# A delta-rule attention with its triangular inverse rearranged: transposes in place of paired products, and a new order of steps

## The chip, the core and the metric

The kernel runs on one core of a Trainium2 chip. A core has a matrix engine (TensorE, in the trace PE for its matmuls and PEld for its weight loads), VectorE (DVE), ScalarE (ACT), GpSimd (POOL) and SyncE (SP), which mostly issues DMAs. Each engine runs its own list of instructions in order and waits for the others by semaphores. Matmuls write to PSUM, eight banks of 128 partitions by 512 fp32 numbers, and DVE or ACT must copy a result from there to SBUF before the matrix engine can use it again. The metric is the device time of one execution in microseconds.

## What is computed

```python
k_n = k / (np.linalg.norm(k, axis=-1, keepdims=True) + 1e-06)
for t in range(S):
    kt, vt, bt = (k_n[:, :, t], v[:, :, t], beta[:, :, t, None])
    y[:, :, t] = np.einsum('bhd,bhde->bhe', q[:, :, t], state)
    v_old = np.einsum('bhde,bhd->bhe', state, kt)
    state = state + bt[:, :, :, None] * np.einsum('bhd,bhe->bhde', kt, vt - v_old)
...
logits = xn @ en.T / tau                      # 8 experts, the best one is taken
h = np.maximum(x[mask] @ w1[e], 0.0)
out[mask] = gate_w[mask, None] * (h @ w2[e])
```

The attention has 4 batches, 8 heads, 768 tokens and head size 48. Its output, 3072 rows of 384, is routed row by row to one of eight experts with 1024 hidden units.

## The kernel before

The recurrence is cut into chunks of 64 tokens. Within a chunk the updates of the state form a triangular system of 64 by 64 for each head, and the kernel inverts its matrix with products. A **unit** is one chunk of two batches: the one batch lies on partitions 0 to 63, the other on 64 to 127, and the 8 heads lie side by side, so that a matrix of a unit is a tile of 128 by 512. There are 24 units (12 chunks, 2 pairs of batches).

A unit passes these steps. `prep` normalises K on POOL and DVE (the roots are `pow` on POOL, L269 and L275). `transposes` makes K and Q transposed. `gram` makes the products K·K and Q·K. The inverse starts with blocks of 8 (`square_t`, `square`, `fourth`, `first_w`) and doubles the block size three times: `level` (L389 copies the lower part out of PSUM under a mask) and `grow`, which makes both W and its transpose T by two products, and at the end `last`. `k_state` and `q_state` read the running state, `solve` applies W, `state` adds to the running state, `outputs` makes the rows of the result, `x_transposes` and `logits` prepare the routing. After every fourth unit `route` sorts the rows to experts.

Every matmul of these steps is 64 by 64 (or 48) by 64 and uses one quarter of the array: rows 0 to 63 or 64 to 127, columns 0 to 63 or 64 to 127. `product` issues two matmuls for each head, one for each batch, on two quarters that lie diagonally (`from_other` and `to_other` choose which diagonal).

What sets the order on the matrix engine is the table `PLAN` with `PERIOD = 8`: each step of unit n has the due time 8·n plus its number, all are sorted, and steps with the same due time are interleaved matmul by matmul (the loop at L578 to L589). So in the running stage two products on different diagonals go side by side. The other engines' lists are left to the scheduler. PSUM has one pool `bank` of six buffers and one `yb` of two.

After the attention, the expert stage (from L595) takes the rows expert by expert in 31 tiles of 128 rows: a gather, 24 matmuls with `w1`, ReLU, 8 with `w2`, and an indirect store. Its weights come by DMA from SP.

Of the kernel before, what the change touches and what calls it, by code (L numbers as in the profile page):

```python
# [8 lines left out]
F32 = mybir.dt.float32  # L9
# [8 lines left out]
LEVELS = (8, 16, 32)  # L18
BLOCK = 8
# [3 lines left out]
def kernel(  # L23
# [33 lines left out]

    nc = tc.nc
# [9 lines left out]
    ps = ctx.enter_context(tc.tile_pool(name="ps", bufs=1, space=bass.MemoryType.PSUM))  # L68
# [3 lines left out]
    def bank(shape):  # L72
        return ps.tile(shape, F32, name="bank", tag="bank", bufs=6)

    def yb():
        t = ps.tile([128, 512], F32, name="yb", tag="yb", bufs=2)
        return t[:, 0:NP * D].rearrange("p (j d) -> p j d", j=NP)
# [32 lines left out]
    att = ExitStack()  # L110
# [35 lines left out]
    id2 = ac.tile([128, 1, C], F32, name="id2")  # L146
    nc.vector.tensor_scalar_mul(id2, id64, 2.0)
    nupper = ac.tile([128, 1, C], F32, name="nupper")
    nc.vector.tensor_tensor(nupper[:, 0, :], col_f, trow_f, op=ALU.is_gt)
    lower = ac.tile([128, C], F32, name="lower")  # L150
    nc.vector.tensor_tensor(lower, col_f, trow_f, op=ALU.is_lt)

    def mask(name, tri, lo, hi):
        m = ac.tile([128, 1, C], F32, name=name)
        nc.vector.scalar_tensor_tensor(out=m[:, 0, :], in0=xor_f, scalar=float(lo), in1=tri,
                                       op0=ALU.is_ge, op1=ALU.mult)
        nc.vector.scalar_tensor_tensor(out=m[:, 0, :], in0=xor_f, scalar=float(hi), in1=m[:, 0, :],
                                       op0=ALU.is_lt, op1=ALU.mult)
        return m.bitcast(I32)

    up8 = mask("up8", nupper[:, 0, :], 0, BLOCK)
    lo8 = mask("lo8", lower, 0, BLOCK)
    below = {s: mask(f"below{s}", lower, s, 2 * s) for s in LEVELS}
    nc.vector.tensor_scalar_mul(nupper, nupper, -1.0)
    hc = [128, H, C]


    def filled(name, bufs, value):

        ts = []  # L170
        for i in range(bufs):
            t = ac.tile(hc, F32, name=f"{name}{i}")
            if value is None:
                nc.gpsimd.memset(t, 0.0)
            elif value == 1.0:
                nc.vector.tensor_copy(t, id64.broadcast_to(hc))
            else:
                nc.vector.tensor_scalar_mul(t, id64.broadcast_to(hc), value)
            ts.append(t)
        return ts  # L180

    KK = filled("KK", 8, None)
    Qp = [filled(f"Qp{i}_", NU, None) for i in range(2)]
    YT = filled("YT", 3, -1.0)
    YI = filled("YI", 2, 1.0)
# [7 lines left out]
    def load_kq(c):  # L193
        K4 = io.tile([128, NU, H, D], F32, name="K4", tag="K4")
        for b in range(B):
            p, u = slice(b % 2 * C, b % 2 * C + C), b // 2
            for dst, src in ((K4[p, u], k), (Qp[c % 2][u][p, :, 0:D], q)):
                nc.sync.dma_start(out=dst, in_=src[b, :, c * C:(c + 1) * C, :].rearrange("h p d -> p h d"))
        return K4

    def load_v(c):
        V4 = io.tile([128, NU, H, D], F32, name="V4", tag="V4", bufs=4)
        for b in range(B):
            p, u = slice(b % 2 * C, b % 2 * C + C), b // 2
            nc.sync.dma_start(out=V4[p, u], in_=v[b, :, c * C:(c + 1) * C, :].rearrange("h p d -> p h d"))
        return V4

    bt = ac.tile([B * H, S], F32, name="bt")
# [5 lines left out]
    K4s, V4s = {0: load_kq(0)}, {}  # L214
# [35 lines left out]

    HALF = (slice(0, C), slice(C, 2 * C))
    UNITS = [dict(n=n, c=n // NU, u=n % NU) for n in range(NC * NU)]
    sqb = {}
    outs = {}

    def hs():
        return range(H)

    def work(name, bufs=2, cols=C):
        return wk.tile([128, H, cols], F32, name=name, tag=name, bufs=bufs)

    def prep(U):
# [5 lines left out]
        K = K4s[c][:, u]  # L270
# [8 lines left out]
        U["K"] = KK[U["n"] % len(KK)]  # L279
        nc.gpsimd.tensor_tensor(U["K"][:, :, 0:D], K, rn.unsqueeze(2).broadcast_to([128, H, D]), op=ALU.mult)  # L280

    def scale_v(U):
        V = V4s[U["c"]][:, U["u"]]
        nc.gpsimd.tensor_tensor(V, V, sqb[U["c"]][:, U["u"]].unsqueeze(2).broadcast_to([128, H, D]), op=ALU.mult)
        U["R"] = V

    def transposes(U):
        U["KT"] = wk.tile([128, NP, 2, 128], F32, name="KT", tag="KT", bufs=6)
        for i, src in enumerate((U["K"], Qp[U["c"] % 2][U["u"]])):
            psT = bank([128, NP, 128])  # L290
            for j in range(NP):
                nc.tensor.transpose(psT[:, j, :], src[:, 2 * j:2 * j + 2, :].rearrange("p h d -> p (h d)"), ident)
            nc.scalar.activation(U["KT"][:, :, i, :], psT, ACT.Copy)

    def gram(U):

        KT, ps = U["KT"], [bank([128, 2, NP, C]) for _ in range(2)]
        groups = []
        for j in range(NP):
            for a in range(2):  # L300
                g = []
                for jj in range(2):
                    pr = slice(jj * C, jj * C + D)
                    for i in range(2):
                        g.append((ps[jj][HALF[i if a else 1 - i], a, j], KT[pr, j, 0, HALF[i]],
                                  KT[pr, j, a, HALF[i]], True))
                groups.append(g)

        def after():
            n = U["n"]  # L310
            U["G"] = wk.tile([128, 2, 2, NP, C], F32, name="G", tag="G", bufs=6)
            U["YT"], U["YI"] = YT[n % len(YT)], YI[n % len(YI)]
            for jj in range(2):
                js = slice(jj * NP, jj * NP + NP)
                nc.scalar.activation(U["G"][:, :, jj], ps[jj], ACT.Copy, scale=-1.0)  # L315
                for t, m in ((U["YT"], up8), (U["YI"], lo8)):
                    nc.vector.copy_predicated(t[:, js], m.broadcast_to([128, NP, C]), ps[jj][:, 0])  # L317
            U["A"] = U["G"][:, 0].rearrange("p jj j t -> p (jj j) t")
            U["M"] = U["G"][:, 1].rearrange("p jj j t -> p (jj j) t")
            nc.gpsimd.tensor_tensor(U["M"], U["M"], nupper.broadcast_to(hc), op=ALU.mult)  # L320
        return groups, after

    def product(p, lhsT, rhs, from_other, to_other):

        groups = []
        for h in hs():
            g = []
            for i in range(2):
                f, o = HALF[1 - i if from_other else i], HALF[1 - i if to_other else i]
                g.append((p[o, h], lhsT[f, h], rhs[f, h], True))  # L330
            groups.append(g)
        return groups

    def evac(eng, out, p):
        if eng == "act":
            nc.scalar.activation(out, p, ACT.Copy)  # L336
        else:
            nc.vector.tensor_copy(out, p)

    def square(U):  # L340
        p = bank(hc)

        def after():
            U["Y2"] = work("Y2")
            nc.vector.tensor_tensor(U["Y2"], p, id2.broadcast_to(hc), op=ALU.add)
        return product(p, U["YT"], U["YI"], True, True), after

    def square_t(U):
        p = bank(hc)

        def after():
            U["Y2T"] = work("Y2T")
            evac("act", U["Y2T"], p)
        return product(p, U["YI"], U["YT"], True, True), after

    def fourth(U):
        p = bank(hc)

        def after():
            U["P"] = work("Y4")  # L360
            nc.vector.tensor_tensor(U["P"], p, id2.broadcast_to(hc), op=ALU.add)
        return product(p, U["Y2T"], U["Y2"], True, False), after

    def first_w(U):
        p = bank(hc)

        def after():
            U["W"] = work("W", 5)
            nc.scalar.activation(U["W"], p, ACT.Copy, scale=-1.0)
        return product(p, U["Y2"], U["YT"], True, False), after  # L370

    def grow(U, eng_w="act"):
        pt, pw = bank(hc), bank(hc)
        P, W = U["P"], U["W"]
        gt, gw = product(pt, W, P, False, True), product(pw, P, W, False, False)

        def after():
            U["T"] = work("T", 3)
            evac("act", U["T"], pt)
            U["W"] = work("W", 5)  # L380
            evac(eng_w, U["W"], pw)
        return [g for gs in zip(gt, gw) for g in gs], after

    def level(U, s):
        p = bank(hc)

# [324 lines left out]
```

## Time and profile before

| | |
|---|---|
| time before, median of 3 runs | 971.53 us (964.52 to 976.65) |
| the profiled execution's own time | 977.07 us |
| its span, first to last instruction | 975.3 us |
| PE matmul busy | 736.1 us, 75%, 18598 instructions |
| PE weight loads | 18598 instructions |
| DVE, ACT, POOL busy | 270.4, 246.2, 262.8 us |
| mean granted TensorE clock | 0.912 of 2.4 GHz |

The profile is of one execution. A wait that is put down to "issue" is one for which the trace shows no semaphore and no other engine's work. A row of a timeline merges neighbouring instructions of one kind; the number behind x counts them. In the trace an fp32 matmul of the source is two MATMUL rows, each with a weight load (LDWEIGHTS) of its own; a transpose is one of each. The trace can miss a few matmul records.

### The profile page before, as it was taken

To read this page: it belongs to the slowest core of one execution; us is meant where nothing else is said; L and a number is where in the kernel's file an instruction comes from. 1 tells how busy PE (TensorE), PEld (TensorE's weight loads), DVE (VectorE), ACT (ScalarE), POOL (GpSimd) and SP (SyncE) were. 2 spreads that over 40 slices of the span, in tenths; PEclk is the share of its full clock that TensorE was granted. 3 is DMA by queue.
4 is the path that set the end of the run, shared out by engine and by line. 5 is a ranking of instruction groups with operands and counts; after the bars stand their busy time and mean duration, and the time that the engine had idled before them with its cause. 6 is when DMAs were issued, how large, how long until landed. Compare 5 with 4: busy or idle time off the path is not lost. (4 is left out here: it accounts for less than half of the span.)

```text
span 975.3 us, 40125 instructions
## 1 busy us (share of the span) xinstructions
PE 736.1 (75%) x18598; PEld 633.3 (65%) x18598; DVE 270.4 (28%) x742; ACT 246.2 (25%) x503; POOL 262.8 (27%) x252
## 2 busy tenths in 40 slices
PE   0476767667667667776876770399999999999995
PEld 0366766667666666665765660377887788877884
DVE  7234434424343435324433322000100010001000
ACT  0233433333432434344333330010011001100110
POOL 6977144252423223211200101111121121111110
PEclk9987999878997999799889895599999999999998
DMA  5232121211222122110100101999999999999960
GB/s 92 48 61 52 27 38 29 60 27 29 45 46 34 29 45 49 24 20 4 37 4 5 36 3 33 372 326 324 322 322 333 325 321 323 327 315 328 318 201 1
DMA packets 135449, 130.13 MB, mean 133 GB/s; under 512 B 85738, under 2 KB 120721, under 8 KB 135282
## 3 DMA queue, kind: packets, MB, share of 16 engines
q1 hardware_dynamic: 128738, 116.55, 39.7%
q0 software_dynamic: 4736, 10.85, 3.3%
q8 instruction: 146, 2.39, 1.1%
q10 hardware_dynamic: 1808, 0.16, 0.1%
q14 instruction: 21, 0.17, 0.1%
HBM read 117.91 MB, written 10.95 MB: 132 GB/s over the span
## 5 line engine op out<-in xcount | busy, mean ns | idle before, releaser
L660 PE MATMUL bank<-xTm,w 128*128 128x128 f32 x1488 | 173.8, 277 | 0.0
L660 PEld LDWEIGHTS bank<-xTm,w 128*128 128x128 f32 x1488 | 171.3, 194 | 0.3
L665 PE MATMUL bank<-w,hT 128*128 128x384 f32 x496 | 165.1, 486 | 0.0
L665 PEld LDWEIGHTS bank<-w,hT 128*128 128x128 f32 x496 | 91.9, 190 | 57.5
L662 ACT ACTIVATE hT<-bank 128x512 f32<-128x512 f32 x62 | 37.0, 597 | 338.5 <-PE bank L660 283.7
L588 PE MATMUL bank<-T,G 64*64 64x64 f32 x2304 | 103.3, 240 | 18.8 <-issue 17.7
L588 PE MATMUL bank<-W,P 64*64 64x64 f32 x2304 | 98.0, 231 | 23.2 <-issue 22.6
L588 PEld LDWEIGHTS bank<-T,G 64*64 64x64 f32 x2304 | 89.8, 152 | 22.8 <-issue 21.0
L667 DVE TENSOR_SCALAR y<-bank,xg 128x384 f32<-128x384 f32 x31 | 19.1, 617 | 305.6 <-PE bank L665 305.6
L588 PEld LDWEIGHTS bank<-W,P 64*64 64x64 f32 x2304 | 84.9, 144 | 28.8 <-issue 27.0
L336 ACT ACTIVATE T<-bank 128x512 f32<-128x512 f32 x72 | 43.1, 598 | 167.6 <-PE bank L588 162.7
L588 PE MATMUL bank<-P,W 64*64 64x64 f32 x1536 | 67.0, 234 | 17.0 <-issue 15.8
L668 POOL DMA_INDIRECT out_dram<-y,ids x31 | 31.3, 1011 | 164.3 <-DVE y L667 161.5
L389 DVE COPY_PREDICATED P<-below,bank 128x512 f32<-128x512 int32 x72 | 53.0, 736 | 71.3 <-PE bank L588 62.3
L588 PEld LDWEIGHTS bank<-P,W 64*64 64x64 f32 x1536 | 58.6, 147 | 20.1 <-issue 18.8
L641 POOL DMA_INDIRECT xg<-x_dram,ids x31 | 30.1, 971 | 136.9 <-DMA ids<-idmap 92.6
L320 POOL TENSOR_TENSOR G<-G,nupper 128x512 f32<-128x512 f32 x24 | 30.5, 1271 | 133.0 <-ACT G L315 122.8
L549 POOL DMA_INDIRECT idmap<-tokid,slot_i x24 | 24.0, 1000 | 107.5 <-DMA idmap<-tokid,slot_i 57.9
L317 DVE COPY_PREDICATED YT<-up,bank 128x256 f32<-128x256 int32 x48 | 21.2, 442 | 98.8 <-ACT G L315 98.8
L588 PE MATMUL bank<-Y,W 64*64 64x64 f32 x768 | 37.3, 253 | 14.8 <-issue 11.2
L588 PE MATMUL bank<-KT 48*64 48x64 f32 x1536 | 38.2, 243 | 11.3 <-issue 10.9
L275 POOL TENSOR_TENSOR rn<-rn,half 128x8 f32<-128x8 f32 x24 | 39.5, 1646 | 24.8 <-DVE rn L274 24.1
(167 smaller groups left out, 1255.2 us busy)
## 6 DMA issues: line engine op xcount, KB each, us to landing
w<-in_moe_w_dram SPq DMA_DIRECT2D x62, 1536.0 KB
x_dram<-xc SPq DMA_DIRECT2D x24, 192.5 KB
K<-in_k_dram SPq DMA_DIRECT2D x48, 96.0 KB
V<-in_v_dram SPq DMA_DIRECT2D x48, 96.0 KB
Qp<-in_q_dram SPq DMA_DIRECT2D x48, 96.0 KB
ids<-idmap SPq DMA_DIRECT2D x31, 0.5 KB
xg<-x_dram,ids POOLq DMA_INDIRECT x31, 6.7
out_dram<-y,ids POOLq DMA_INDIRECT x31, 6.9
```

The lines of the kernel that those rows point to most:

```text
L275: nc.gpsimd.tensor_tensor(out=rn, in0=rn, in1=half[:, 0], op=ALU.pow)
L317: nc.vector.copy_predicated(t[:, js], m.broadcast_to([128, NP, C]), ps[jj][:, 0])
L320: nc.gpsimd.tensor_tensor(U["M"], U["M"], nupper.broadcast_to(hc), op=ALU.mult)
L336: nc.scalar.activation(out, p, ACT.Copy)
L389: nc.vector.copy_predicated(U["P"], below[s].broadcast_to(hc), p)
L549: nc.gpsimd.indirect_dma_start(out=idmap[:, :], out_offset=bass.IndirectOffsetOnAxis(ap=slot_i[:, g:g + 1], axis=0), in_=tokid[:, c - 1 + ...
L588: nc.tensor.matmul(out_, lhsT=lhsT, rhs=rhs, start=start, stop=True, skip_group_check=True)
L641: nc.gpsimd.indirect_dma_start(out=x, out_offset=None, in_=x_dram[:, :], in_offset=bass.IndirectOffsetOnAxis(ap=ids[:, 0:1], axis=0))
L660: nc.tensor.matmul(psH[:, i, :], lhsT=w1[:, j, (f + i) * 128:(f + i + 1) * 128], rhs=xT[:, j, :], start=(j == 0), stop=(j == KC - 1))
L662: nc.scalar.activation(hT[:, f:f + 4, :], psH, ACT.Relu)
L665: nc.tensor.matmul(psO, lhsT=hT[:, f, :], rhs=w2[:, f, :], start=(f == 0), stop=(f == NF - 1))
L668: nc.gpsimd.indirect_dma_start(out=out[:, :], out_offset=bass.IndirectOffsetOnAxis(ap=ids[:, 0:1], axis=0), in_=y, in_offset=None, bounds_ ...
```

## The change

The inverse now starts at blocks of 2 instead of 8: `square_t`, `square`, `fourth` and `first_w` are gone, and W starts from `gram`'s result under a mask. There are four levels (2, 4, 8, 16) instead of three. `grow` makes W alone; T, its transpose, comes from four transposes of 128 by 128 (`t_flip`), and A is transposed once in the same way (`a_flip`). The last doubling, to 64, is not made; the right-hand side is solved in three steps instead (`solve1`, `solve2`, `solve3`). `gram` makes both of its products in one matmul with 128 columns. `product` now uses all four quarters of the array within one step (two heads, two batches), into two banks. Steps are no longer interleaved; the plan gives each of the 24 slots of a period one step, and steps that write to `pair` (three buffers of two banks) alternate with steps that write to `bank` (two buffers of one bank). K, Q and V are loaded per unit instead of per chunk. The expert stage gets a PSUM pool of its own, `acc`, with eight buffers.

```diff
-LEVELS = (8, 16, 32)
-BLOCK = 8
+LEVELS = (2, 4, 8, 16)
...
-        return ps.tile(shape, F32, name="bank", tag="bank", bufs=6)
+        return ps.tile(shape, F32, name="bank", tag="bank", bufs=2)
+    def pair(shape):
+        t = ps.tile([128, 2, 512], F32, name="pair", tag="pair", bufs=3)
...
+    def load(U, dst, src):
+        t0 = U["c"] * C
+        for i in range(2):
+            nc.sync.dma_start(out=dst[i * C:(i + 1) * C],
+                              in_=src[2 * U["u"] + i, :, t0:t0 + C, :].rearrange("h p d -> p h d"))
...
+        KT, p = U["KT"], pair([NP, 2, C])
         for j in range(NP):
+            for jj in range(2):
+                pr = slice(jj * C, jj * C + D)
+                for i in range(2):
+                    mm(p[HALF[i], jj, j], KT[pr, j, 0, HALF[i]], KT[pr, j, :, HALF[i]])
...
+    def flip(src):
+        p = bank(jc)
+        for j in range(NP):
+            nc.tensor.transpose(p[:, j].rearrange("p r c -> p (r c)"), src[:, j].rearrange("p r c -> p (r c)"), ident)
+        return p
+    def a_flip(U):
+        p = flip(U["A"][0])
+        U["A"][1] = work("AJ", 3)
+        nc.scalar.activation(U["A"][1], p, ACT.Copy)
+        U["T"] = T2[U["n"] % 2]
+        nc.vector.copy_predicated(U["T"], below[1].broadcast_to(jc), p)
+    def t_flip(U, eng):
+        p = flip(U["W"])
+        U["T"] = work("T", 3)
+        eng(U["T"], p)
...
+    def product(lhsT, rhs):
+        p = pair([NP, C])
+        for j in range(NP):
+            for a in range(2):
+                for b in range(2):
+                    mm(p[HALF[b], a, j], lhsT[HALF[a], j, b], rhs[HALF[a], j, b])
...
+    def grow(U):
+        p = product(U["P"], U["W"])
+        U["W"] = work("W", 5)
+        act_copy(U["W"], p)
...
+    def apply(lhsT, rhs):
+        p = bank([128, H, D])
+        for h in range(H):
+            for i in range(2):
+                mm(p[HALF[i], h], lhsT[HALF[i], h // 2, h % 2], rhs[HALF[i], h])
+        return p
+    def solve1(U):
+        p = apply(U["W"], U["R"])
+        U["Z1"] = narrow("Z1")
+        nc.scalar.activation(U["Z1"], p, ACT.Copy, scale=first)
+    def solve2(U):
+        p = apply(U["A"][0], U["Z1"])
+        nc.vector.scalar_tensor_tensor(out=U["R"], in0=p, scalar=second, in1=U["R"], op0=ALU.mult, op1=ALU.add)
+    def solve3(U):
+        p = apply(U["W"], U["R"])
+        U["Z"] = narrow("Z")
+        act_copy(U["Z"], p)
...
-    PERIOD = 8
+    PERIOD = 24
     PLAN = [
-        (-24, prep), (8, scale_v), (-19.5, transposes), (-15.5, gram),
-        (-10, square_t), (-6, square), (-3, fourth), (0, first_w), (3, grow),
-        (6, lambda U: level(U, 8)), (9, grow), (12, lambda U: level(U, 16)), (15, lambda U: grow(U, "dve")),
-        (18, lambda U: level(U, 32)), (21, last), (21.5, k_state), (23.5, q_state), (24, solve),
-        (26.5, state), (28, outputs), (31.5, x_transposes), (33.5, logits),
+        (-72, load_kq), (-42, prep), (-30, load_v), (10, scale_v),
+        (-23, lambda U: transposes(U, 0)), (-19, lambda U: transposes(U, 1)), (-12, gram), (-5, a_flip),
+        (0, lambda U: level(U, 2, 1)), (4, grow), (9, lambda U: t_flip(U, nc.vector.tensor_copy)),
+        (14, lambda U: level(U, 4, 0)), (18, grow), (23, lambda U: t_flip(U, nc.vector.tensor_copy)),
+        (30, lambda U: level(U, 8, 1)), (34, grow), (39, lambda U: t_flip(U, act_copy)),
+        (44, lambda U: level(U, 16, 0)), (50, grow),
+        (32, q_state), (40, k_state), (55, solve1), (59, solve2), (65, solve3), (70, state), (69, outputs),
+        (75, x_transposes), (85, logits), (90, route_after),
     ]
```

First place: the matrix engine's list in the running stage of the attention, a part of a unit's period. Of before (W and P are the inverse and its next factor, YT and Y belong to the start of a later unit, S and KT to `q_state`, R to `solve`; x counts matmuls of the source):

```order
L588 MATMUL bank<-P_1_190,W 64x64 x2
L588 MATMUL bank<-W,P_1_190 64x64 x2
...
L482 MATMUL bank<-ident,xc 128x128 x3
L588 MATMUL yb<-S_196,KT 64x48 x16
L588 MATMUL bank<-R,W 64x48 x2
L588 MATMUL bank<-YT_176,Y_5602 64x64 x2
...
L588 MATMUL bank<-KT 64x64 x32
```

And of the change (a row with `ident` is a block of transposes, `W,P` is `grow`, `T,AJ` or `T,G` is `level`, `R,W` is `solve1` or `solve3`, `Z_1897,G` is `solve2`):

```order
L268 MATMUL pair<-W,P_1_196 64x64 x16
L444 MATMUL bank<-ident,xc 128x128 x3
L268 MATMUL pair<-W_1_176,P_1_184 64x64 x16
L304 MATMUL bank<-ident,QQ_170 128x128 x4
L268 MATMUL pair<-T,AJ 64x64 x16
L268 MATMUL bank<-R,W 64x48 x16
L268 MATMUL pair<-S_198,KT 64x48 x16
L329 MATMUL bank<-ident,W 128x128 x4
L268 MATMUL pair<-W,P_0_190 64x64 x16
L268 MATMUL bank<-Z_1897,G 64x48 x16
L268 MATMUL pair<-KT 64x128 x16
```

The alternation of two products is gone: each step stands alone, the products with R, W and Z among them, and a block of transposes stands between products about every fourth row.

Second place: VectorE's list in the running stage. Of before (P is `level`'s masked copy, Y belongs to the start of a unit, the rn rows are `prep`):

```order
L274 TENSOR_REDUCE rn<-Ksq 128x8
L276 TENSOR_SCALAR rn<-rn 128x8
L277 RECIPROCAL rn<-rn 128x8
L278 TENSOR_TENSOR rn<-rn,sqb 128x8
L389 COPY_PREDICATED P_0_188<-below_143,bank 128x512
L361 TENSOR_TENSOR Y_5309<-bank,id_128 128x512
```

And of the change:

```order
L342 COPY T<-bank 128x512
L286 TENSOR_REDUCE rn<-Ksq 128x8
L359 COPY_PREDICATED P_0_182<-below_138,pair 128x512
L288 TENSOR_SCALAR rn<-rn 128x8
L289 RECIPROCAL rn<-rn 128x8
L290 TENSOR_TENSOR rn<-rn,sqb 128x8
L359 COPY_PREDICATED P_1_192<-below_144,pair 128x512
L342 COPY T<-bank 128x512
L406 SCALAR_TENSOR_TENSOR R<-bank,second,R 128x384
```

In both lists one masked copy stands directly behind the rn rows, of which the second waits for POOL's `pow`. In the change another masked copy stands between the sum of squares and that wait.

## Rows read from the trace of the kernel before

**Rows 1.** Windows: us, PE, PEld, DVE, ACT, POOL busy (x), clock, DMA, GB/s.
```profile
100.00:540.00 440.00, 311.68 (x13818) 284.30 (x13812) 169.46 (x456) 168.47 (x360) 116.84 (x103) 0.90 0.16 30
...
627.00:975.30 348.30, 338.51 (x2073) 271.05 (x2071) 33.16 (x61) 37.04 (x62) 59.51 (x60) 0.99 0.87 294
```

**Rows 2.** Waits of PE in 100:540: us in total, times, longest.
```profile
PE bank L588 <- issue: 95.9, 88, 3.2
PE yb L588 <- issue: 16.2, 16, 2.5
PE bank L535 <- DVE den L524: 9.3, 4, 2.7
PE bank L588 <- DVE P L389: 2.5, 2, 1.3
```

**Rows 3.** DMA queues in 100:540: packets, MB, share of 16 engines.
```profile
q8 instruction: 108, 1.77, 1.8%
```

**Rows 4.** Windows cut where a PE wait for "issue" ends.
```profile
500.70:504.46 3.76, 2.13 (x128) 2.00 (x128) 0.00 (x0) 0.98 (x2) 0.00 (x0) 1.00 0.02 4
504.46:508.03 3.57, 3.34 (x127) 3.06 (x128) 1.49 (x5) 2.06 (x4) 1.28 (x1) 0.74 0.02 5
...
511.88:515.62 3.74, 2.08 (x128) 1.96 (x128) 1.44 (x2) 1.66 (x5) 0.00 (x0) 1.00 0.02 4
...
519.64:523.11 3.47, 2.72 (x128) 2.35 (x128) 0.69 (x1) 1.81 (x4) 0.00 (x0) 1.00 0.02 5
```

**Rows 5.** Costliest groups by line: xcount, then busy us, mean ns, idle before.
```profile
L588 PE MATMUL bank<-T,G 64*64 64x64 f32 x2304 | 103.3, 240 | 18.8 <-issue 17.7 <-DVE W L338 1.0
L389 DVE COPY_PREDICATED P<-below,bank 128x512 f32<-128x512 int32 x72 | 53.0, 736 | 71.3 <-PE bank L588 62.3 <-PE yb L588 8.7
L336 ACT ACTIVATE T<-bank 128x512 f32<-128x512 f32 x72 | 43.1, 598 | 167.6 <-PE bank L588 162.7 <-PE bank L482 4.9
L275 POOL TENSOR_TENSOR rn<-rn,half 128x8 f32<-128x8 f32 x24 | 39.5, 1646 | 24.8 <-DVE rn L274 24.1 <-DVE rn L278 0.8
...
L667 DVE TENSOR_SCALAR y<-bank,xg 128x384 f32<-128x384 f32 x31 | 19.1, 617 | 305.6 <-PE bank L665 305.6
...
L292 PE MATMUL bank<-ident,KK 128*128 128x128 f32 x96 | 17.9, 311 | 17.1 <-POOL KK L280 14.8 <-issue 2.2
...
L338 DVE COPY W<-bank 128x512 f32<-128x512 f32 x24 | 16.6, 692 | 33.8 <-PE bank L588 28.4 <-PE bank L482 5.4
```

**Rows 6.** Timeline of PE where steps stand alone: start, us, what, xcount, idle before.
```profile
576.88 0.64 PE L588 MATMUL bank<-S,KT 48*64 48x48 f32 x30
577.45 0.55 PE L482 MATMUL bank<-ident,xc 128*128 128x128 f32 x3
577.92 0.68 PE L588 MATMUL yb<-S,KT 48*64 48x48 f32 x32
578.42 1.17 PE L588 MATMUL bank<-R,W 64*64 64x48 f32 x32
579.52 0.52 PE L588 MATMUL bank<-enT,xT 128*64 128x8 f32 x12
580.26 1.13 PE L588 MATMUL yb<-Z,G 64*64 64x48 f32 x32 [0.22 <-ACT Z L336]
581.93 0.55 PE L482 MATMUL bank<-ident,xc 128*128 128x128 f32 x3 [0.53 <-ACT xc L336]
583.05 0.52 PE L588 MATMUL bank<-enT,xT 128*64 128x8 f32 x12 [0.58 <-ACT xT L484]
```

**Rows 7.** Timeline of PE at a granted clock of 0.5.
```profile
465.43 1.05 PE L588 MATMUL bank<-Z,KK 64*64 64x48 f32 x32
466.26 0.34 PE L588 MATMUL bank<-Y,W 64*64 64x64 f32 x2
```

**Rows 8.** Windows before and at a fall of the granted clock.
```profile
295.00:299.00 4.00, 1.82 (x92) 1.48 (x92) 0.76 (x1) 0.60 (x1) 0.00 (x0) 1.00 0.39 37
299.00:313.00 14.00, 11.94 (x351) 10.78 (x355) 3.41 (x8) 4.35 (x8) 4.81 (x5) 0.58 0.14 23
```

More of the change, by code (lines that the diff above doesn't have):

```diff
@@ L253, with mm, work, narrow @@
     HALF = (slice(0, C), slice(C, 2 * C))
[L254 to L262, printed above, removed]
+    sqb, outs = {}, {}
+    def mm(out_, lhsT, rhs, start=True):
+        nc.tensor.matmul(out_, lhsT=lhsT, rhs=rhs, start=start, stop=True, skip_group_check=True)
+    def work(name, bufs=2):
+        return wk.tile(jc, F32, name=name, tag=name, bufs=bufs)
+    def narrow(name, bufs=2):
+        return wk.tile([128, H, D], F32, name=name, tag=name, bufs=bufs)
     def prep(U):
@@ L279, in prep, with transposes @@
         U["K"] = KK[U["n"] % len(KK)]
+        U["K"] = U["K"].rearrange("p j r d -> p (j r) d")
         nc.gpsimd.tensor_tensor(U["K"][:, :, 0:D], K, rn.unsqueeze(2).broadcast_to([128, H, D]), op=ALU.mult)
     def scale_v(U):
-        V = V4s[U["c"]][:, U["u"]]
+        V = U["R"]
         nc.gpsimd.tensor_tensor(V, V, sqb[U["c"]][:, U["u"]].unsqueeze(2).broadcast_to([128, H, D]), op=ALU.mult)
[L285 to L293, printed above, removed]
+    def transposes(U, a):
+        if a == 0:
+            U["KT"] = wk.tile([128, NP, 2, 128], F32, name="KT", tag="KT", bufs=4)
+        p, src = bank([128, NP, 128]), U["Q" if a else "K"]
+        for j in range(NP):
+            nc.tensor.transpose(p[:, j], src[:, 2 * j:2 * j + 2, :].rearrange("p h d -> p (h d)"), ident)
+        act_copy(U["KT"][:, :, a], p)
@@ L309, in after @@
[L309 to L382, printed above, removed]
@@ L384, in level @@
-    def level(U, s):
-        p = bank(hc)
-        def after():
-            U["P"] = PP[s][U["n"] % 2]
-            nc.vector.copy_predicated(U["P"], below[s].broadcast_to(hc), p)
-        return product(p, U["A"], U["T"], True, False), after
-    def last(U):
-        p = bank(hc)
-        groups = product(p, U["P"], U["W"], False, False)
-        def after():
-            U["W"] = work("W", 5)
-            evac("act", U["W"], p)
-        return groups, after
-    def of_state(U, a):
-        p = [yb() if a else bank([128, NP, D]) for _ in range(2)]
-        groups = []
-        for j in range(NP):
-            g = []
@@ new lines, in level, with by_head, of_state @@
+    def level(U, s, by):
+        p = product(U["A"][by], U["T"])
+        U["P"] = PP[s][U["n"] % 2]
+        nc.vector.copy_predicated(U["P"], below[s].broadcast_to(jc), p)
+    def grow(U):
+        p = product(U["P"], U["W"])
+        U["W"] = work("W", 5)
+        act_copy(U["W"], p)
+    def by_head(t):
+        return t.rearrange("p (j jj) d -> p j jj d", jj=2)
+    def of_state(U, a):
+        p = pair([NP, D])
+        for j in range(NP):
+            for jj in range(2):
+                pr = slice(jj * C, jj * C + D)
+                for i in range(2):
+                    mm(p[HALF[i], jj, j], U["KT"][pr, j, a, HALF[i]], S_u[U["u"]][pr, j, i])
+        return p.rearrange("p jj j d -> p j jj d")
@@ L415, in k_state @@
     def k_state(U):
+        V = U["R"]
+        U["R"] = narrow("R")
         if U["c"] == 0:
[L417 to L425 removed]
@@ L453, in state @@
         S_ = S_u[U["u"]]
-        def after():
-            for i in range(2):
-                nc.vector.tensor_tensor(S_[:, :, i], p[i], S_[:, :, i], op=ALU.add)
-        return groups, after
+        nc.vector.tensor_tensor(S_, p.rearrange("p i j d -> p j i d"), S_, op=ALU.add)
     def outputs(U):
@@ L575 @@
-    events.sort(key=lambda e: e[:2])
-    with tc.manual_schedule(engines={mybir.EngineType.PE}):
-        while events:
-            now = [events.pop(0)]
-            while events and events[0][0] == now[0][0]:
-                now.append(events.pop(0))
-            done = [r for r in (e[2]() for e in now) if r is not None]
-            groups = [g for g, _ in done]
-            while any(groups):
-                for g in groups:
-                    if g:
-                        for out_, lhsT, rhs, start in g.pop(0):
-                            nc.tensor.matmul(out_, lhsT=lhsT, rhs=rhs, start=start, stop=True,
-                                             skip_group_check=True)
-            for _, after in done:
-                after()
+        (-72, load_kq), (-42, prep), (-30, load_v), (10, scale_v),
```

209 lines of the change are left out of this document (95 added, 114 removed).

## The prediction, made before the changed kernel was run

> **What bounds the kernel now.** I first cut the span into stages. From 100 to 540 us the attention runs full: PE is busy 311.68 of 440 us, DVE 169.46, ACT 168.47 and POOL 116.84, so none of the four fills the stage [rows 1]. The expert stage after 627 us is another matter: PE is busy 338.51 of 348.30 us there [rows 1], the change alters nothing in it but the number of PSUM buffers, and I take it as it is.
>
> Next I asked what PE waits for between 100 and 540 us. It idles 128 us. Of these 95.9 + 16.2 = 112.1 us, in 104 waits, are put down to "issue", that is to nothing the profile shows; the router's sums cost 9.3 us and the masked copies of `level` 2.5 us [rows 2]. So the copies are in time and something else is late.
>
> Third, I cut windows at the ends of those waits. Each holds 128 matmuls and 128 weight loads, one record aside, whether PE is busy 2.08 us of it or 3.34 us, and each lasts 3.47 to 3.76 us [rows 4]. In the 440 us the instruction queue moved 1.77 MB in 108 packets, 16.4 KB each [rows 3], and 13818 matmuls over 128 are 108.0. So PE gets its program in pieces of 256 instructions, one piece takes 440/108 = 4.07 us on average, and a piece whose array work is shorter ends in a wait. The supply of instructions bounds the attention.
>
> **The change, part by part.** In instructions: 2304 rows for `level`, at 24 units, 3 levels and 16 matmuls, are two per matmul; 96 rows for K's transposes at 4 a unit are one per transpose [rows 5]. Each has a weight load, so a matmul of the source costs four instructions and a transpose two. Per unit, from 342 matmuls and 11 transposes, the change takes away 16 of `gram`, 64 of the start at blocks of 8 and 48 that made T; it adds 16 for the fourth level and 32 for two more solve steps (four growths of W stay four, `last` being one), and 16 transposes. That leaves 262 and 27. In instructions this is 1390 before and 1102 after, or 5.43 and 4.30 pieces per unit. Over the whole attention the order holds 8124 matmuls and 273 transposes before, 6204 and 657 after: 129 pieces against 102.
>
> At 4.07 us a piece a unit takes 5.43 x 4.07 = 22.1 us now, and would take 4.30 x 4.07 = 17.5 us.
>
> But the array's own work grows. Prices at full clock come from the drain, where steps stand alone [rows 6]. A step on four quarters has 32 matmul rows in 0.68 us; less the 0.22 us of the last one that is (0.68 - 0.22)/31 = 14.8 ns each. A step on one diagonal (`outputs`) has (1.13 - 0.22)/31 = 29.4 ns. Three transposes take from the last start before them (576.88 + 0.64 - 0.22 = 577.30) to the next step's start at 577.92: 0.62 us, of which a fourth adds at most (0.55 - 0.22)/2 = 0.16; I take 0.75 us for four. `logits` takes about 0.6 us.
>
> Before, the products are interleaved on both diagonals, so all 672 rows but `logits` run at 14.8 ns: 9.9 us, plus 8 transposes in a run (1.2), 3 alone (0.6) and `logits` (0.6), makes 12.3 us per unit. After: eight products, `q_state`, `k_state` and `state` have 352 rows, `gram` 32 with 128 columns. The trace has no such matmul; its price lies between 14.8 (columns free) and 29.6 ns (columns double), and I take the upper, as `gram`'s two halves cost that now. That is 416 x 14.8 = 6.2 us. `solve1`, `solve2`, `solve3` and `outputs` lose their partners: 128 x 29.4 = 3.8 us. Six blocks of four transposes and one of three cost 5.1 us, `logits` 0.6: 15.7 us, or 15.2 if `gram`'s added columns were free. A piece then holds 15.7/4.30 = 3.65 us of array work, where it held 12.3/5.43 = 2.27 us; supply and array are now nearly level.
>
> At the half clock, 1.2 GHz, the array takes twice as long: 32 rows start within 0.83 us [rows 7], 26 ns each. A mean granted clock of 0.90 [rows 1] is a fifth of the time at the low level. Before, a piece then took 4.5 us of array, hardly over the supply; after, it takes 7.3. The granted clock is 0.58 from 299 to 313 us, behind a stretch in which PE was busy 1.82 of 4.00 us [rows 8]; with the array work at 3.65 of some 4.2 us a piece there should be fewer such stretches, and I take a tenth of the time. The mean piece is then 1/(0.9/4.07 + 0.1/7.3) = 4.26 us, and a unit 4.30 x 4.26 = 18.3 us.
>
> Here a rule speaks against the change. The rows show PE waiting 112.1 us for "issue" at every 256th instruction [rows 2, 4]. The Trainium skill (Runtime: NRT & Kernel Launch, section Instruction fetch mechanics) says that instructions are refilled in 16 KiB blocks of 256, and that crossing a block is mostly hidden. The trace agrees with the block and not with the hiding. By that rule fewer instructions would give nothing by themselves.
>
> The other edits I cost at nothing while they are covered. Copies: `level` to `grow` is now 4 of 24 slots, 4 x 18.3/24 = 3.05 us, where it was 3 of 8, 8.3 us. It has to hold the matmuls' 0.47 us, their 0.22 us tail and a masked copy of 0.736 us [rows 5], 1.4 us in all, which leaves 1.6 us for queueing on DVE. DVE's work per unit is six masked copies, two of 0.692, four of 384 columns at about 0.617 [rows 5] and some 2.8 us of small ones: 11 us of 18.3. ACT copies at 0.598 us [rows 5], and its 14 or so per unit are 8.6 us. PSUM buffers come round after six slots (`pair`) or four (`bank`), 4.6 and 3.05 us, by the same copies. The loads are the same 144 transfers, issued per unit and three periods ahead, behind the router's stores on SP as before; POOL's list keeps its operations.
>
> A unit's chain has about four more links (two more solves, `a_flip`, one more level with its growth and flips, less the four steps at the start). A link in the drain takes 1.7 us or 1.1 us [rows 6]. It is paid once, where the pipeline fills and empties: 7 us.
>
> Sum, against the profiled execution's own 977.1 us: 977.1 - 24 x (22.1 - 18.3) + 7 = 893 us. That execution is 0.6% above the median of the runs shown (971.5), so the forecast is 888 us. With a piece between 3.9 and 4.5 us a unit takes 16.8 to 19.4 us and the time is 850 to 915 us: the likeliest case's own range.
>
> **The rivals.** *The supply alone still sets the pace.* If a piece's array work hides wholly and the pace falls toward the 3.47 us of the shortest window [rows 4], the array at 15.7 to 16 us per unit is the floor: 977.1 - 24 x 6.2 + 7 = 835, against the median 830 us. For it: windows at full clock stay near 3.5 to 3.8 us whatever they hold. Against it: the mean is 4.07.
>
> *Copies come late.* In DVE's order a masked copy stands behind the rn rows, which wait for POOL's `pow` of 1.646 us [rows 5]. If PE pays that once and a little more per unit, 2.2 us, a unit takes 20.5 us: 946, against the median 940 us. For it: distances of 3.05 us instead of 8.3. Against it: PE waited 2.5 us for such copies in the whole running stage [rows 2].
>
> *The clock stays low, and the kernel gets slower.* With 0.6 of the time at 1.2 GHz the mean piece is 1/(0.4/4.07 + 0.6/7.3) = 5.55 us and a unit 23.8 us: 977.1 + 41 + 7 = 1025, or 1020 us. It decides from about 0.45 of the time, where the piece costs what it saves (5.1 us). For it: the array at the low clock is the bound at once. Against it: only a fifth of the time is low now, with a PE that idles more [rows 1].
>
> *The waits are not the supply's.* If something else spaced the waits, only array work would count: 24 x (15.7 - 12.3) + 7 = 89 us more, 1066, or 1060 us. Against it: 108 packets for 108.0 pieces [rows 1, 3]. It is also where the rule of the Trainium skill (Runtime: NRT & Kernel Launch, Instruction fetch mechanics) would end, at these 1060 us.
>
> **How the numbers follow.** I give the forecast 0.62, the supply alone 0.10, the late copies 0.15, the low clock 0.08 and the array alone 0.05. The predicted time is 888 us. The range 835 to 950 us takes in the forecast's, half of the supply case and most of the late copies, some 0.79. A difference of 2%, 19.4 us, is about what a measurement of this kernel tells from no change. Faster by more, under 952 us: the forecast, the supply alone and most of the late copies, 0.83. Slower by more: most of the last two, 0.10. Within: 0.07.
>
> **What would show it.** In the changed profile about 102 instruction packets before the expert stage; a unit every 18.3 us, with PE busy over 85% of the running stage; waits for "issue" well under half of 112 us; a lone diagonal step at 29 ns per row and `gram` at about 29 ns; blocks of transposes at 0.75 us; few waits of PE for DVE. The forecast fails if the period is 22 us or more with fewer packets (then the waits were not the supply's), if the granted clock is below 0.8 in the running stage, or if PE's waits name DVE or ACT for more than 50 us.

## The result, and the profile of the changed kernel

The changed kernel takes 903.5 us (median; 903.1 to 907.9) where the kernel before takes 970.4 us in the runs beside it: a ratio of 0.932, 95% interval 0.925 to 0.939. The forecast was 888 us, its range 835 to 950. The profiled span fell from 975.3 to 901.9 us at a mean granted clock of 0.94.

The running stage and the expert stage (length, then busy time of PE, PEld, DVE, ACT and POOL, clock, DMA share, GB/s), beside [rows 1]:

```profile
100.00:460.00 360.00, 315.80 (x10380) 275.19 (x10377) 185.45 (x411) 157.13 (x307) 123.43 (x108) 0.95 0.20 37
560.00:902.00 342.00, 332.08 (x2039) 264.55 (x2037) 32.62 (x60) 36.42 (x61) 58.51 (x59) 0.99 0.87 293
```

PE is busy 88% of the running stage, where it was 71%. A unit now has 262 x 2 + 27 = 551 matmul rows, so 10380 rows in 360 us are 19.1 us per unit; before, with 342 x 2 + 11 = 695, it was 22.1. What PE waits for in that stage (us, times, longest), beside [rows 2]:

```profile
PE pair L268 <- DVE P L359: 15.1, 10, 3.7
PE pair L268 <- DVE ssx L467: 11.6, 4, 4.6
PE pair L268 <- issue: 8.4, 10, 1.8
PE bank L268 <- issue: 4.3, 3, 2.9
PE pair L268 <- DVE oh L475: 3.0, 4, 0.8
```

The waits for "issue", 112.1 of 440 us before, are 12.9 of 360. In their place stand 30 us of waits for DVE. The queue of instructions up to 555 us, after [rows 3]:

```profile
q8 instruction: 102, 1.67, 1.4%
```

Two stretches of the trace show where the DVE waits come from. First POOL and DVE around a wait of PE (start, duration, in brackets the idle time before and who ended it):

```profile
227.11 2.90 POOL L281 TENSOR_TENSOR sqb<-betaT,half 128x16 f32<-128x16 f32 x1
229.97 0.83 POOL L293 TENSOR_TENSOR KK<-k_in,rn 128x384 f32<-128x384 f32 x1
230.75 1.01 POOL L465 TENSOR_TENSOR ssx<-ssx,half 128x4 f32<-128x4 f32 x1
...
231.80 0.17 DVE L466 TENSOR_SCALAR ssx<-ssx 128x4 f32<-128x4 f32 x1 [4.89 <-POOL ssx L465]
231.88 0.55 DVE L286 TENSOR_REDUCE rn<-Ksq 128x8 f32<-128x384 f32 x1
232.34 0.71 DVE L359 COPY_PREDICATED P<-below,pair 128x512 f32<-128x512 int32 x1
...
233.10 1.10 PE L268 MATMUL pair<-W,P 64*64 64x64 f32 x32 [4.61 <-DVE ssx L467]
```

POOL's root of beta, 2.90 us at every second unit, delays KK and the router's `ssx`; DVE stands 4.89 us at `ssx`, with the masked copy P behind it, and PE 4.61 us for that copy. The wait costs more than its own length. The granted clock is 1.00 in the stretch before it and 0.51 in the one behind it (length, busy times, clock, as above), where the product of 32 rows takes 1.10 us; at the full clock such a product takes 0.69 us:

```profile
226.10:228.50 2.40, 2.40 (x72) 1.85 (x71) 0.80 (x2) 1.06 (x3) 2.22 (x2) 1.00 0.02 7
233.10:236.50 3.40, 3.40 (x77) 2.95 (x78) 1.28 (x5) 1.19 (x2) 1.89 (x2) 0.51 0.16 31
```

Between 100 and 460 us the clock is at its low level (1.2 GHz) in seven stretches, 34 us in all. Six of them begin within a wait for P or `ssx` or less than 1 us behind one.

The second stretch is the start, POOL again:

```profile
22.77 11.49 POOL L281 TENSOR_TENSOR sqb<-betaT,half 128x16 f32<-128x16 f32 x4
34.22 0.83 POOL L297 TENSOR_TENSOR v_in<-v_in,sqb 128x384 f32<-128x384 f32 x1
35.01 1.74 POOL L293 TENSOR_TENSOR KK<-k_in,rn 128x384 f32<-128x384 f32 x2
```

Four such roots stand ahead of the first KK, and PE's first transposes of K begin at 35.9 us. The kernel before has the same four, for 11.50 us.

### The profile page after: what moved, and what is told of

Same layout as the page of the kernel before. It is cut to its first block, busy times and chain, and to the rows that moved or that the text cites. A ratio compares the mean times of both kernels' runs of the same rounds, so it can differ in the third digit from the quotient of the medians.

```text
span 901.9 us, 33180 instructions
## 1 busy us (share of the span) xinstructions
PE 749.8 (83%) x15142; PEld 627.8 (70%) x15142; DVE 296.3 (33%) x703; ACT 238.0 (26%) x453; POOL 261.9 (29%) x250
## 5 line engine op out<-in xcount | busy, mean ns | idle before, releaser
L610 PE MATMUL acc<-xTm,w 128*128 128x128 f32 x1488 | 172.4, 276 | 0.0
L610 PEld LDWEIGHTS acc<-xTm,w 128*128 128x128 f32 x1488 | 169.9, 193 | 0.3
L615 PE MATMUL acc<-w,hT 128*128 128x384 f32 x496 | 165.1, 486 | 0.0
L615 PEld LDWEIGHTS acc<-w,hT 128*128 128x128 f32 x496 | 91.9, 190 | 57.5
L268 PE MATMUL pair<-W,P 64*64 64x64 f32 x3072 | 75.4, 233 | 44.3 <-DVE P L359 22.9
L268 PEld LDWEIGHTS pair<-W,P 64*64 64x64 f32 x3072 | 60.7, 141 | 60.0 <-DVE P L359 28.4
L359 DVE COPY_PREDICATED P<-below,pair 128x512 f32<-128x512 int32 x96 | 69.2, 721 | 25.4 <-PE pair L268 25.4
L345 ACT ACTIVATE W<-pair 128x512 f32<-128x512 f32 x96 | 57.3, 597 | 73.2 <-PE pair L268 71.3
L268 PE MATMUL bank<-Z,G 64*64 64x48 f32 x1536 | 55.8, 220 | 6.3 <-issue 5.4
L268 PE MATMUL bank<-R,W 64*64 64x48 f32 x1536 | 59.3, 229 | 0.7 <-ACT W L345 0.6
L600 PEld LDWEIGHTS acc<-ident,xg 128*128 128x128 f32 x93 | 12.3, 146 | 48.5 <-issue 36.2
```

What stands on the lines that cost most here:

```text
L268: nc.tensor.matmul(out_, lhsT=lhsT, rhs=rhs, start=start, stop=True, skip_group_check=True)
L345: nc.scalar.activation(out_, in_, ACT.Copy)
L359: nc.vector.copy_predicated(U["P"], below[s].broadcast_to(jc), p)
L600: nc.tensor.transpose(psX[:, j, :], x[:, j * 128:(j + 1) * 128], ident)
L610: nc.tensor.matmul(psH[:, i, :], lhsT=w1[:, j, (f + i) * 128:(f + i + 1) * 128], rhs=xT[:, j, :], start=(j == 0), stop=(j == KC - 1))
L615: nc.tensor.matmul(psO, lhsT=hT[:, f, :], rhs=w2[:, f, :], start=(f == 0), stop=(f == NF - 1))
```

## Experiments

The theory (S): the attention of before goes at the pace of its instructions, a piece of 256 in about 4.07 us; the changed kernel has array and supply nearly level, and its missing microseconds are copies late behind DVE's waits for POOL. The rivals: only array work counts (A), or supply alone still sets the pace. Sizes of a unit below are worked out as above, from the matmul rows of a window.

**Instructions without array work.** `e1` and `e2` add matmuls of one column ahead of those of one level (the lines here and below are those of the changed kernel; the kernel before has the like, at `level` 8).

```diff
+        for j in range(NP):
+            for a in range(2):
+                for b in range(2):
+                    for _ in range(extra):
+                        mm(p[HALF[b], a, j, 0:1], lhsT[HALF[a], j, b], rhs[HALF[a], j, b, 0:1])
...
-        p = product(U["A"][by], U["T"])
+        p = product(U["A"][by], U["T"], 2 if s == 2 else 0)
```

`e1`, on the kernel before. Expected: 

> The kernel before, with 32 matmuls of one column added per unit ahead of the real ones of `level` 8, into places that the real ones then overwrite: 128 PE instructions more per unit, half a piece of 256, and next to no array work. If the supply of instructions bounds the attention of before: 0.5 x 4.07 x 24 = 49 us more. If only array work counts: at most 64 rows x 14.8 ns x 24 = 23 us more, and less than that if one column costs less than 64.

`e2`, on the changed kernel. Expected: 

> The changed kernel with the same 32 matmuls of one column per unit (128 PE instructions, half a piece). If its array is now nearly level with the supply (unit of 19.1 us, 4.30 pieces): 4.80 pieces x 4.07 = 19.5 us of supply per unit, so 10 to 23 us more in all, less than half of what the kernel before pays. If the supply alone still sets the pace: 0.5 x 4.44 x 24 = 53 us more.

**Array work without instructions.** `e3` and `e4` widen matmuls to 128 columns; what is too much is overwritten by the next.

```diff
-                    mm(p[HALF[b], a, j], lhsT[HALF[a], j, b], rhs[HALF[a], j, b])
+                    js = slice(j, min(j + 2, NP))
+                    mm(p[HALF[b], a, js], lhsT[HALF[a], j, b], rhs[HALF[a], js, b])
```

`e3`, on the kernel before. Expected: 

> The kernel before, where 14 of 16 matmuls in ten products per unit (`level`, `grow`, `last`) have 128 columns instead of 64; the second 64 are overwritten by the next matmul. Same instructions, 280 rows per unit of double width: 280 x 14.8 ns = 4.1 us more array work per unit. If the supply bounds: array 16.4 us in a unit of 22.1, so 0 to 20 us more. If only array work counts: 24 x 4.1 = 99 us more.

`e4`, on the changed kernel. Expected: 

> The changed kernel, where 12 of 16 matmuls in its eight products per unit have 128 columns: 192 rows of double width, 2.84 us more array work per unit, same instructions. If its array is nearly the bound now: array 15.7 + 2.8 = 18.5 us per unit beside the waits for late copies, 40 to 68 us more in all. If the supply alone sets the pace: 0 to 15 us more.

Measured beside a kernel before of 973.6 us: `e1` 1016.1 us (ratio 1.043, 1.034 to 1.052), 43 us more; `e3` 983.8 us (1.010, 1.003 to 1.017), 10 us more. The running stage and the instruction queue, first of `e1`, then of `e3`:

```profile
100.00:540.00 440.00, 339.26 (x14009) 314.50 (x14001) 158.47 (x430) 158.30 (x335) 114.49 (x101) 0.86 0.16 31
...
q8 instruction: 109, 1.79, 1.9%
```

```profile
100.00:540.00 440.00, 378.88 (x13733) 352.60 (x13729) 169.90 (x451) 169.60 (x357) 116.17 (x103) 0.97 0.16 31
...
q8 instruction: 107, 1.75, 1.8%
```

With PE busy 312, 339 or 379 of 440 us, the queue brings 108 [rows 3], 109 or 107 packets: one in 4.07, 4.04 and 4.11 us. Array work goes into the pauses, instructions lengthen the stage. A falls: by it 99 us were due for `e3`, and at most 23 us for `e1`. The lower clock of `e1`, 0.86 for 0.90, is not what costs the 43 us: PE still idles 101 of the 440 us there, 87 of them for "issue", and a packet takes no longer.

The changed kernel did not answer as any theory said. `e2` takes 977.0 us and `e4` 982.0 us, 73 and 78 us more than the 903.5. The unit is 22.8 us (9721 rows of 615 to a unit) and 23.8 us (8321 rows of 551). In both, PE waits longest for a copy behind DVE's rn rows. Here are the running stage and the first row of PE's waits of `e2`, then of `e4`, both in 100 to 460 us, and for `e4` two rows of DVE's waits and three of its timeline:

```profile
100.00:460.00 360.00, 299.72 (x9721) 262.29 (x9713) 158.63 (x364) 132.10 (x257) 111.78 (x97) 0.88 0.19 36
...
PE pair L268 <- DVE rn L290: 37.7, 11, 7.0
```

```profile
100.00:460.00 360.00, 296.69 (x8321) 263.90 (x8325) 153.22 (x339) 125.59 (x247) 110.64 (x96) 0.92 0.18 33
...
PE pair L268 <- DVE rn L290: 58.6, 16, 6.2
...
DVE rn L288 <- POOL rn L287: 28.0, 16, 1.8
...
DVE rn L286 <- POOL KK L293: 15.8, 9, 3.5
...
241.44 0.55 DVE L286 TENSOR_REDUCE rn<-Ksq 128x8 f32<-128x384 f32 x1 [1.09 <-POOL KK L293]
243.74 0.78 DVE L288 TENSOR_SCALAR rn<-rn 128x8 f32<-128x8 f32 x1 [1.75 <-POOL rn L287]
...
244.67 0.67 DVE L360 COPY_PREDICATED P<-below,pair 128x512 f32<-128x512 int32 x1
```

The edits moved DVE's list, which is not written by hand: the waiting rn row L288 now stands directly behind L286 and ahead of the masked copy, where in the changed kernel a P stood between. The waits are 2.4 and 3.9 us per unit. They are not the whole loss: the changed kernel itself waits for DVE 30 us in its 18.8 units, 1.6 us each, and the units grew by 3.7 and 4.7 us. The granted clock fell as well, from 0.95 to 0.88 and 0.92, so a quarter and a sixth of the stage ran at the low level instead of a tenth. So `e2` and `e4` tell little of supply or array, and what share of their loss is copies, clock, instructions or array was not told apart.

**The root of beta off POOL.** `e5` and `e8` take it once, ahead of the attention, on ScalarE; `e6` issues it twice.

```diff
+    nc.scalar.activation(sqb_all, betaT, ACT.Sqrt)
...
-            nc.gpsimd.tensor_tensor(out=sqb[c], in0=betaT[:, c], in1=half, op=ALU.pow)
+            sqb[c] = sqb_all[:, c]
```

`e5`, on the changed kernel. Expected: 

> The changed kernel with the square root of beta taken once, ahead of the attention, by one ScalarE instruction; POOL's `sqb` power of 2.90 us, which stands in its queue at every second unit, is gone. In the profile of the changed kernel PE waits 26.7 of 360 us for DVE's masked copy P and for `ssx`, and in both DVE had waited for POOL behind that power. If this power is what makes those copies late: 20 to 35 us less. If the wait only passes to the next one in the queue (the power of `rn`, 1.64 us at every unit): 0 to 10 us less.

`e6`, on the changed kernel. Expected: 

> The changed kernel with POOL's `sqb` power issued twice in a row, 2.9 us more of POOL at every second unit. If it stands in the path by way of DVE's copies: 12 x 2.9 = 35 us more, or somewhat less. If POOL is off the path: no difference.

`e8`, on the kernel before. Expected: 

> The kernel before with the square root of beta taken once ahead of the attention, the same edit. There PE waited 2.5 of 440 us for a masked copy, so if the supply of instructions bounds it: within 8 us of no difference. If POOL's power delays the kernel before as well: 15 us less or more.

`e5` takes 871.3 us (ratio to before 0.897, 0.893 to 0.901), 32 us less than the changed kernel; `e6` 938.6 us (0.967, 0.962 to 0.972), 35 us more. `e5` in the running stage, with its waits for DVE:

```profile
100.00:460.00 360.00, 324.99 (x10908) 282.23 (x10900) 195.30 (x443) 162.79 (x318) 108.80 (x103) 0.98 0.20 38
...
PE pair L270 <- DVE ssx L468: 5.7, 4, 1.7
PE pair L270 <- DVE P L360: 4.2, 9, 0.7
```

Both came as expected. P and `ssx` fell from 26.7 to 9.9 us, the granted clock rose from 0.95 to 0.98, and the unit fell to 360/(10908/551) = 18.2 us. But the running stage is only part of the gain: the first transposes of K stand at 24.7 us instead of 35.9 us, 11 us earlier, which is the 11.49 us of four roots at the start. At the 1500th matmul row, near 100 us, the profiled `e5` is 16 us ahead, of 30 us at its end. `e6` has the mirror of it: the first transposes at 47.4 us, 11.5 us later, and 9925 rows in the running stage, 20.0 us per unit.

I had not counted the start, and with it `e8` missed its expectation: 949.9 us (0.978, 0.975 to 0.982), 22 us less where at most 8 were expected. The start, now at 25.0 us instead of 35.5, gives 10.5 of them. Some 5 us more come while the pipeline fills: at the 1500th matmul row `e8` is 15.7 us ahead (83.0 us for 98.6). From 100 to 460 us `e8` has 11362 rows where the kernel before has 11242, 22.0 us per unit for 22.3, which is 6 us over 24 units; from 100 to 540 us the two hardly differ (13834 rows for 13818). So POOL's power costs the kernel before too, but mostly ahead of its running stage.

**DVE and POOL in an order written by hand.** `e7`, `e9` and `e11`, all with beta's root ahead as in `e5`, cut `prep` in three and `route` in four, six and nine steps, each some slots behind what it needs. The plan's lines below are those of `e7`, whose `route4` ends with the four indirect transfers; in `e9` these stand by themselves at slot 117, in `e11` at 117, 125, 133 and 141.

```diff
-        (-72, load_kq), (-42, prep), (-30, load_v), (10, scale_v),
+        (-72, load_kq), (-52, prep), (-44, prep1), (-36, prep2), (-30, load_v), (10, scale_v),
...
-        (75, x_transposes), (85, logits), (90, route_after),
+        (75, x_transposes), (85, logits), (89, route_after), (95, lambda U: late(U, route2)), (101, lambda U: late(U, route3)),
+        (106, lambda U: late(U, route4)),
...
-    with tc.manual_schedule(engines={mybir.EngineType.PE}):
+    with tc.manual_schedule(engines={mybir.EngineType.PE, mybir.EngineType.DVE, mybir.EngineType.Pool}):
```

`e7`. Expected: 

> The changed kernel with `sqb` taken ahead, `prep` cut into three steps and `route` into four, each some slots behind the one it needs, and the order of DVE and POOL written out as that of PE is, so that DVE's small instructions stand where their inputs should be there. If late copies behind DVE's waits for POOL are what the unit of 19.1 us has over the 18.3 forecast: 18.0 to 18.5 us per unit, 865 to 885 us, and PE's waits for DVE under 10 of 360 us. If the array and the supply alone make 19.1 us: no difference, 895 to 910 us.

885.6 us (0.910, 0.905 to 0.915): worse than `e5`, and the unit is 19.4 us (10241 rows in 360 us) where 18.0 to 18.5 were expected. PE's waits for P went down, to 3.8 us, but a new one leads:

```profile
PE bank L311 <- POOL KK L300: 35.4, 4, 9.8
```

`e9`. Expected: 

> The hand-ordered kernel once more, with `route` in six steps: POOL's four indirect transfers now stand 9 slots behind the last DVE step that they wait for, and behind the next unit's `KK`, ahead of which they stood in the run before. There every fourth unit took 27 to 28 us, with PE waiting up to 9.8 us for `KK`, and the others 15.5 to 17.7. If that wait is all that the fourth units have more: 16 to 17.5 us for each unit, 4 x 10 us less, 840 to 855 us, with a piece of instructions every 3.8 to 4.0 us. If a unit can't go below 17.5 us because a piece takes 4.07 us: 865 us or more.

870.4 us (0.895, 0.891 to 0.899): 15 us less than `e7` where 30 to 45 were expected, and in the other branch, 865 us or more. POOL shows the router's indirect transfers each waiting for the one before, and DVE's rn behind them:

```profile
157.79 0.98 POOL L542 DMA_INDIRECT idmap<-tokid,slot_i  x1 [5.40 <-DMA idmap<-tokid,slot_i]
162.96 0.96 POOL L542 DMA_INDIRECT idmap<-tokid,slot_i  x1 [4.19 <-DMA idmap<-tokid,slot_i]
167.65 0.96 POOL L542 DMA_INDIRECT idmap<-tokid,slot_i  x1 [3.73 <-DMA idmap<-tokid,slot_i]
168.63 1.68 POOL L291 TENSOR_TENSOR rn<-rn,half 128x8 f32<-128x8 f32 x1
...
170.34 0.80 DVE L295 TENSOR_SCALAR rn<-rn 128x8 f32<-128x8 f32 x1 [7.48 <-POOL rn L291]
```

`e11`. Expected: 

> The hand-ordered kernel with the router's four indirect transfers issued 8 slots apart instead of in a row. In the run before, each waited for the landing of the one before it (5.40, 4.19 and 3.73 us on POOL), the power of `rn` stood behind all four, DVE waited 7.48 us for it, and every fourth unit took 21 to 25 us where the others took 16 to 17.3. If that is all: 16 to 17.5 us for every unit, 20 to 30 us less than that kernel, 840 to 852 us. If the transfers' waits only move to the POOL work between them: 860 to 870 us.

857.9 us (0.885, 0.878 to 0.892), the fastest of all kernels here, though neither the 840 to 852 expected nor the 860 to 870 of the rival. Its running stage, its packets and PE's waits from 100 to 400 us:

```profile
100.00:400.00 300.00, 277.85 (x9334) 241.58 (x9331) 163.15 (x393) 140.28 (x275) 111.32 (x105) 0.99 0.23 42
...
q8 instruction: 74, 1.21, 1.8%
...
PE bank L270 <- issue: 7.7, 14, 1.4
PE pair L270 <- issue: 7.7, 13, 1.3
PE pair L270 <- DVE P L366: 4.1, 4, 1.3
```

A unit takes 300/(9334/551) = 17.7 us, and 74 packets in 300 us are one in 4.05 us, the pace of before. With the copies in time the waits are again mostly "issue", but they are only 15.4 of 300 us: array and supply are now close together. Four units run without any wait of PE, in 15.4 to 15.5 us. One of them lies between these two blocks of K's transposes, 134.62 - 119.18 = 15.44 us:

```profile
119.18 0.66 PE L311 MATMUL bank<-ident,KK 128*128 128x128 f32 x4
...
134.62 0.66 PE L311 MATMUL bank<-ident,KK 128*128 128x128 f32 x4
```

Seven others, all those that neither hold the router's sums nor follow right behind them, take 1.3 to 2.7 us more. Row by row, 11.2 of the 12.3 us that these seven take beyond 15.44 us stand within three rows of one fixed row in 128, as the waits of the kernel before do. So there the supply is the bound again. `e11` with more instructions, which would test it directly, was not run.

**The array, cleanly.** `e10` is `e9` with the wide matmuls of `e4`. Expected: 

> The same hand-ordered kernel with 12 of 16 matmuls of each product at 128 columns: 192 rows of double width, 2.84 us more array work per unit, same instructions. If the array is the bound of the changed kernel once the copies are in time: 2.3 to 3.0 us more per unit, 55 to 72 us more than the hand-ordered kernel beside it. If the instructions' supply is the bound: 0 to 25 us more.

895.0 us (0.919, 0.915 to 0.924), 25 us more than `e9`: the upper end of the lower branch. A product step at 128 columns, then the transposes of K of two successive units (PE: start, busy time, rows):

```profile
226.46 1.00 PE L270 MATMUL pair<-W,P 64*64 64x128 f32 x32
227.39 0.55 PE L452 MATMUL bank<-ident,xc 128*128 128x128 f32 x3
...
208.00 0.66 PE L311 MATMUL bank<-ident,KK 128*128 128x128 f32 x4
...
225.87 0.66 PE L311 MATMUL bank<-ident,KK 128*128 128x128 f32 x4
```

And the same step at 64 columns in `e9`:

```profile
231.16 0.69 PE L270 MATMUL pair<-W,P 64*64 64x64 f32 x32
231.79 0.55 PE L451 MATMUL bank<-ident,xc 128*128 128x128 f32 x3
```

Start to start the step takes 0.93 us for 0.63: 0.30 us more, so eight of them 2.4 us. A unit that here goes from 208.00 to 225.87, 17.9 us, without a wait of PE in it, therefore has 15.5 us of array work without the widening, as `e11` shows it directly. The prediction's sum was 15.7. Of the 24 x 2.4 = 58 us of added array work 25 show in the time. Part of the rest went into pauses that `e9` has: its waits for "issue" are 15.2 of 300 us, those of `e10` 2.4.

**The order alone.** `e12` puts rn's waiting rows back ahead of P in `e11`.

```diff
-        (-72, load_kq), (-52, prep), (-44, prep1), (-36, prep2), (-30, load_v), (10, scale_v),
+        (-72, load_kq), (-52, prep), (-44, prep1), (-43.5, prep2), (-30, load_v), (10, scale_v),
```

Expected: 

> The kernel of the run before, with the three small DVE instructions of `rn` (L295 to L297) moved from behind the masked copy P, T's copy and the update of R to directly behind the reduction L290, so that DVE waits there for POOL's power of 1.64 us ahead of that P. No work is added. The runs with extra and with wider matmuls had this order, as the trace shows (L288, L289, then P), and PE waited 37.7 and 58.6 of 360 us for DVE behind `rn`. If such an order is what cost them 2 us and more per unit: 15 to 53 us more than the kernel without it (0.6 to 2.2 us per unit, the lower end if the 1.5 us that a masked copy has to spare take up most of the wait), with PE waiting for DVE P or rn. If the wait is hidden: 0 to 5 us.

861.8 us (0.893, 0.887 to 0.898), 4 us more, or 7 with each beside its own kernel before, and overlapping intervals: hidden, or nearly. DVE does wait for the power at every unit, PE does not for DVE:

```profile
DVE rn L295 <- POOL rn L291: 30.1, 17, 1.8
```

So that order alone is not what `e2` and `e4` paid. There DVE waited for POOL twice in a row, at L286, where the trace names KK, and at L288 for the power, later in the slots, and the clock was lower. Which of these decides wasn't told apart.

## Why the prediction was right, and where it was off

- **Supply bounds the kernel before**: shown by `e1` and `e3`. The rule of the Trainium skill (Runtime: NRT & Kernel Launch, Instruction fetch mechanics), that crossing a block is mostly hidden, does not hold for this stream: 43 us for half a piece per unit is 43/24/0.5 = 3.6 us a piece. A piece's time varies more than the 3.47 to 3.76 us that I read in [rows 4]: the two windows left out there last 3.85 and 4.02 us.
- **129 pieces to 102**: 102 packets up to 555 us, as counted.
- **15.7 us of array per unit**: 15.44 in `e11`, 15.5 by `e10`. In the changed kernel a lone diagonal step has 28.6 ns per row and `gram` 27.6, for 29.4 and 29.6. A block of four transposes and a product, costed at 0.75 + 0.47 us, take 186.43 - 185.21 = 1.22 us in the changed kernel:

```profile
185.21 0.66 PE L329 MATMUL bank<-ident,W 128*128 128x128 f32 x4
185.80 0.69 PE L268 MATMUL pair<-T,AJ 64*64 64x64 f32 x32
186.43 0.66 PE L304 MATMUL bank<-ident,KK 128*128 128x128 f32 x4
```

- **Low clock a tenth of the time**: the granted clock is 0.95 in the running stage, a tenth, but in part by luck. I tied the low clock to the pauses that the supply leaves, and six of the seven low stretches stand beside a wait for a late copy. With the copies more in time the clock is 0.98 (`e5`) and 0.99 (`e11`). It does not simply follow PE's busy time: 0.90 before with PE busy 71%, 0.97 in `e3` with 86%, but 0.86 in `e1` with 77%. And I let the array take twice as long at the low clock, where [rows 7] has 26 ns for 14.8, 1.75 times.
- **PE busy over 85%, "issue" well under half, few waits for DVE**: 88%, and 12.9 us of 360. The waits for DVE were not few: 30 us, below the 50 us that I had named as a failure.
- **Seven microseconds for fill and drain**: not seen. From the first transposes of K to the last router sum the attention took 550.6 us before (35.5 to 586.1) and 478.0 after (35.9 to 513.9); less 24 units of 22.1 or 19.1 that leaves about 20 us in both.
- **Copies at nothing while covered: the step that failed.** The unit takes 19.1 us, not 18.3, which is 19 us over 24 units; with the 7 not paid, that leaves 12 us too little in the sum. The time lies 11 us above the sum for the profiled execution (903.6 against 893) and 15 above the forecast for the median. The cover of 1.6 us that I worked out between `level` and `grow` holds for one wait of DVE. POOL's queue was costed at nothing ("keeps its operations"), yet its root of beta, at every second unit, stands ahead of what DVE needs: DVE waits up to 6.0 us at rn's reduction and up to 4.9 us at `ssx`, and the clock falls behind PE's waits for the copies. The late-copy rival named the engine and the queue rightly but the wrong power (rn's instead of beta's) and too high a price, 2.2 us per unit for 0.8. `e5` removes that power and gets 18.2 us per unit. That this is the forecast's 18.3 is luck in part: `e5` still waits 15 of 360 us for DVE, and its clock is low for a twenty-fifth of the time, not a tenth.
- **Supply alone, or a low clock**: neither came. With the copies in time, `e11` takes 17.7 us per unit and 4.05 us per packet, not the 15.9 us per unit of the first rival's 835 us, though single units do reach 15.44 us.

## What to carry to other kernels

Count instructions where PE's waits for "issue" repeat at a fixed count; there, array work that replaces instructions is nearly free up to the packet's pace (10 us for the 99 us of `e3`), and `e1` and `e3` are the pair of edits that tells. Once that bound is lifted, look for the next one in what other engines' queues hold ahead of the copies, small operations first: here a 2.9 us power ahead of a 0.2 us row was worth 32 us, a third of it at the start. A wait can cost twice, once as idle time and once by the low clock behind it. And where a scheduler orders an engine, an edit elsewhere can move its list, as in `e2` and `e4`, so an experiment's other orders have to be read too.

## What the runs showed of the hardware

Doubling a matmul's columns on a quarter of the array adds 12.5 ns to a row of some 15 (0.30 us over 24 rows, `e10` beside `e9`), so 128 columns cost less than twice 64. POOL's power takes 2.90 us for 16 columns, 1.64 for 8 and 1.01 for 4. Four indirect transfers to one DRAM tensor, each made to wait for the landing of the one before, start 4.7 to 6.6 us apart on POOL (`e9`). Where the copies are in time, the mean pace of instruction packets hardly depends on the work in them: 4.04 to 4.11 us in four kernels whose PE was busy from 71% to 93%. Where copies are late, fewer packets come: one in 4.44 us in the changed kernel (81 in 360 us) and in 4.24 us in `e5` (85). Over single units the pace is not even: 15.44 us for the 4.30 pieces of a unit are 3.6 us a piece.
